# An attention and two mixture-of-experts layers on one core: GpSimd instructions cut in two, and the queues in another order at four places

## The chip, the cores and the metric

One NeuronCore of a Trainium2 chip runs the whole program. The metric is the device time of one execution in microseconds (us); lower is better.

## What is computed

Three layers follow each other, all in float32. The reference, cut to what matters:

```python
# 1. attention, 4 batches x 8 heads, 576 tokens, head size 64
scores = scale * q @ k.T
scores = where(scores >= max(scores) - tau, scores, -1e9)
attn = exp(scores - max(scores)); attn /= sum(attn) + 1e-9
x = (attn @ v)                       # 2304 tokens x 512 columns
# 2. eight experts, each token goes to one
e = argmax(x @ w_gate); gate = softmax(x @ w_gate)[e]
x = gate * (relu(x @ w1[e]) @ w2[e])       # 512 -> 1024 -> 512
# 3. four experts, each token goes to all
p = domain_probs / (sum(domain_probs) + 1e-9)
out = sum over e of p[:, e] * (relu(x @ v1[e]) @ v2[e])
```

## The kernel before

Almost every product of matrices in it is made of three matmuls. A float32 operand is split into a high part, rounded to the fast format (`fp32r`), and a low part, the operand minus the high part. Then high*high + high*low + low*high are summed in PSUM. Each operand is split by two instructions: a copy that rounds, mostly on ScalarE (ACT), and a subtraction on GpSimd (POOL) or VectorE (DVE). Weights arrive as a tile `raw` of 128x1024 and become the tile `hl` (or `v2hl`): high in `hl[:, 0]`, low in `hl[:, 1]`.

All engines run their instructions in the order of the program text (`tc.manual_schedule()`), so the text sets the order, and an instruction that waits holds up those behind it on its engine.

**Attention (0 to about 357 us).** The loop runs over 144 steps `t`, nine for each of 16 head pairs `p`. In step `t`, TensorE makes the scores of the step after (`mm_s`, tile `s`, L733 and L734), transposes of q and k for a later pair (L583), and the transposes of the masked exponentials of four steps ago (`transp`, L781 to L790). VectorE reads the scores (`maxx`, tile `sb`, L742) and two steps later makes the masked row (`mask`, tile `P`, L762). The product with v (PV, L816 and L822) is cut in two halves of tokens per pair, each half of five items: one matmul, and four pairs of matmuls. These ten items wait in a list `pv`. `PG = 3` takes from it every third step, 4, 3 and 3 items. After a half, an item `ev` copies the sum out of PSUM (`outT`, L833, VectorE) in the step that follows, and frees its PSUM bank. When all four pairs of a batch are done, another list `xq` runs the routing (`route`): logits, argmax, places, and a scatter of token rows (`free_scatter`, an indirect DMA issued by POOL).

In steps 140 and 143 the first two weight tiles of layer 2 are split on POOL alone (`dosplit(i, "g", "g")`: L358 makes the high part, L360 the low part).

**Layer 2 (to about 587 us).** 72 units of weights, one tile each; `dosplit(i + 3)` splits a tile three units ahead. The low part is on VectorE for five of eight units and on POOL for the rest.

**Layer 3 (from 588 us).** 48 steps `j`: three phases `ph` of 768 tokens, 16 steps each (four experts by four blocks of the hidden width). In a step, `l1` makes the first matrix product by Strassen's scheme: seven products `prod` of sums of blocks (PSUM tiles X, Y, Z, W, U; L1356 to L1358, six matmuls of 384 columns each), put together on VectorE (`q`, `r`, `c`, L1365) and split for the second product by `relu` (L1370 on ACT, L1371 on VectorE, tile `g`). `l2` makes the second product (L366 to L368, 36 matmuls of 512 columns). The inputs of the seven products are the tiles `yc`: `in_parts` makes high (ACT, L1222) and low (VectorE, L1181) of three blocks and four sums of blocks of `y`. `sums` makes the sums (`t`, and one in place in `y`). Weights for step `j + 2` are prepared by `prep1` (sums `sx` on POOL, L1199 and L1181, splits `hl`), those of the second product by `prep2` (`v2hl`, L1212 and L1181). L1181 is the line of a helper `sub`, used on both engines.

In `l1`, the first product goes to X, ACT copies it to `p` (L1375), and a second product is added into X later, so TensorE waits there for the copy `p`. `mid` is what the caller wants done behind that copy. In step 0 it is `first_blocks`, which makes four of the seven `yc`. The sequence `l1(1)`, `l2(0)`, ... is turned over so that two `l1` stand back to back at three places: steps 1 and 2, 16 and 17, 32 and 33.

The lines that set this order at the places of the change, before:

```python
            if pv and (t % PG == 1 or t > 9 * last):
...
        def first_blocks():
            for _ in range(3):
                next(ahead)
            for _ in parts2(0, (4, 5, 3)):
                pass
            prep2(0)
            next(ahead)
            for _ in parts2(0, (2,)):
                pass
```

## Time and profile before

| | |
|---|---|
| median of 3 runs | 1360.22 us (1359.86 to 1360.77) |
| the profiled execution | 1361.25 us, of which the span of instructions is 1358.8 us |
| TensorE (PE) busy | 1323.6 us, 97% |
| GpSimd (POOL) busy | 890.4 us, 66% |
| VectorE (DVE) busy | 865.9 us, 64% |
| ScalarE (ACT) busy | 653.8 us, 48% |

Times in a row are counted from the start of the span. A row of the timeline is start, duration, engine, line, instruction, and in brackets the idle time of the engine before it and what ended it. A matmul's recorded duration overlaps that of the next, so the pace of TensorE is read from start to start, and its waits from the idle time in brackets. DVE, ACT and POOL rows follow one another in order.

### The profile page before, as it was taken

The page shows a single profiled execution, that of the slowest core. Times are in us where ns is not written, and L with a number is a line of the kernel's source. Part 1 is how long each engine was busy: PE and PEld are TensorE (multiplying, and loading weights), DVE is VectorE, ACT ScalarE, POOL GpSimd, SP SyncE. Part 2 cuts the span into 40 slices and gives each one's busy share as a digit, 9 for nine tenths or more (in the row PEclk, how much of TensorE's full clock was granted, in tenths as well). Part 3 has the DMA queues.
Part 4 walks back from the last instruction along what each step waited for, and adds up shares of the span by engine and source line. Part 5 has one row for each costly group of instructions (what it writes and reads, how often), then busy time and mean ns, then how long its engine had stood idle before and what let it go on. Part 6 is the DMA issues. An engine that isn't in the chain of part 4 may idle for free.

```text
span 1358.8 us, 22300 instructions
## 1 busy us (share of the span) xinstructions
PE 1323.6 (97%) x8120; PEld 1169.4 (86%) x8120; DVE 865.9 (64%) x1705; ACT 653.8 (48%) x1239; POOL 890.4 (66%) x945
## 2 busy tenths in 40 slices
PE   8999999999999999979999999999999999999997
PEld 7777777776899999968999998898999989999986
DVE  8878778777843333545566667666666676655664
ACT  7887786866454455633333334333333343333331
POOL 8876766845385444658666766777677657666642
PEclk8999999999999999989999999999999999999999
DMA  5551111103584556522221112222112222222201
GB/s 153 167 158 57 58 55 62 37 17 110 165 239 148 167 177 203 172 64 78 76 80 62 63 62 67 84 99 78 63 62 76 80 68 80 78 70 78 78 16 47
DMA packets 131696, 127.52 MB, mean 94 GB/s; under 512 B 17920, under 2 KB 110080, under 8 KB 131584
## 3 DMA queue, kind: packets, MB, share of 16 engines
q1 hardware_dynamic: 128128, 116.55, 27.4%
q0 software_dynamic: 3456, 9.51, 1.8%
q8 instruction: 66, 1.08, 0.3%
q14 instruction: 46, 0.38, 0.1%
HBM read 107.61 MB, written 18.42 MB: 93 GB/s over the span
## 4 chain that ended last, share of the span: by engine, by line
PE 68%; issue 3%; POOL 2%; ACT 1%; DVE 1%; POOLq 0%; ACTq 0%; DVEq 0%
PE w L366 14%; PE w L367 14%; PE w L368 14%; PE w L1356 8%; PE w L1358 8%; PE w L1357 8%; PE w L395 1%; PE t L822 0%; DVE g L1371 0%; DVE P L762 0%; POOL out_dram L192 0%; DVE c L1365 0%; POOL hl L360 0%; POOL v2hl L1181 0%; ACT v2hl L1212 0%
## 5 line engine op out<-in xcount | busy, mean ns | idle before, releaser
L1356 PE MATMUL w<-yc,hl 128*128 128x384 f32 x672 | 227.3, 338 | 13.5 <-DVE r L1365 6.5
L1181 POOL TENSOR_TENSOR v2hl<-raw,v2hl 128x1024 fp32r<-128x1024 f32 x48 | 116.0, 2416 | 172.2 <-ACT v2hl L1212 172.2
L1357 PE MATMUL w<-yc,hl 128*128 128x384 f32 x672 | 226.5, 337 | 0.5 <-DVE yc L1181 0.5
L1358 PE MATMUL w<-yc,hl 128*128 128x384 f32 x672 | 226.7, 337 | 0.0
L368 PE MATMUL w<-v2hl,g 128*128 128x512 f32 x576 | 225.3, 391 | 0.0
L366 PE MATMUL w<-v2hl,g 128*128 128x512 f32 x576 | 225.2, 391 | 0.0
L367 PE MATMUL w<-v2hl,g 128*128 128x512 f32 x576 | 224.9, 390 | 0.0
L1420 DVE SCALAR_TENSOR_TENSOR y<-w,big,y 128x512 f32<-128x512 f32 x252 | 179.3, 745 | 51.0 <-PE w L368 50.9
L1370 ACT ACTIVATE g<-c 128x384 fp32r<-128x384 f32 x144 | 75.9, 527 | 191.9 <-DVE c L1365 191.9
L360 POOL TENSOR_TENSOR hl<-raw,hl 128x1024 fp32r<-128x1024 f32 x44 | 107.6, 2446 | 90.6 <-ACT hl L356 55.5
L1371 DVE SCALAR_TENSOR_TENSOR g<-c,g 128x384 fp32r<-128x384 f32 x144 | 111.6, 775 | 62.5 <-ACT g L1370 56.3
L745 POOL TENSOR_SCALAR nm<-nm,sc 128x1 f32<-128x1 f32 x144 | 92.6, 643 | 81.9 <-DVE sb L742 56.0
L1356 PEld LDWEIGHTS w<-yc,hl 128*128 128x128 f32 x672 | 127.0, 189 | 17.3 <-ACT p L1375 7.1
L1212 ACT CAST v2hl<-raw 128x1024 fp32r<-128x1024 f32 x48 | 50.5, 1053 | 188.6 <-PE w L368 188.6
L762 DVE SCALAR_TENSOR_TENSOR P<-sb,nm,E 128x576 f32<-128x576 f32 x144 | 133.5, 928 | 9.1 <-issue 3.0
L1357 PEld LDWEIGHTS w<-yc,hl 128*128 128x128 f32 x672 | 127.1, 189 | 2.6 <-DVE yc L1181 0.8
L368 PEld LDWEIGHTS w<-v2hl,g 128*128 128x128 f32 x576 | 108.3, 188 | 23.6 <-DVE g L1371 0.5
L366 PEld LDWEIGHTS w<-v2hl,g 128*128 128x128 f32 x576 | 108.5, 188 | 21.7 <-ACT g L1370 0.6
L1358 PEld LDWEIGHTS w<-yc,hl 128*128 128x128 f32 x672 | 126.9, 189 | 0.0
L367 PEld LDWEIGHTS w<-v2hl,g 128*128 128x128 f32 x576 | 108.4, 188 | 21.4
L1181 POOL TENSOR_TENSOR hl<-sx,hl 128x1024 fp32r<-128x1024 f32 x48 | 115.6, 2409 | 13.8 <-ACT hl L1196 13.8
L1181 POOL TENSOR_TENSOR hl<-raw,hl 128x512 fp32r<-128x512 f32 x96 | 97.2, 1034 | 41.7 <-ACT hl L1196 41.7
(292 smaller groups left out, 3151.4 us busy)
## 6 DMA issues: line engine op xcount, KB each, us to landing
raw<-in_moe_w_dram SPq DMA_DIRECT2D x168, 512.0 KB
xs<-zrow SPq DMA_DIRECT2D x32, 256.0 KB
xrow<-xs SPq DMA_DIRECT2D x18, 256.0 KB
kt<-in_k_dram SPq DMA_DIRECT2D x16, 256.0 KB
qt<-in_q_dram SPq DMA_DIRECT2D x16, 256.0 KB
vt<-in_v_dram SPq DMA_DIRECT2D x16, 256.0 KB
kt<-in_k_dram SPq DMA_DIRECT2D x16, 32.0 KB
qt<-in_q_dram SPq DMA_DIRECT2D x16, 32.0 KB
```

What stands on the lines that cost most here:

```text
L360: e.tensor_tensor(hl[:, 1, :], raw, hl[:, 0, :].bitcast(F32), op=ALU.subtract)
L366: nc.tensor.matmul(o, lhsT=aH, rhs=bH, start=first, stop=False)
L367: nc.tensor.matmul(o, lhsT=aH, rhs=bL, start=False, stop=False)
L368: nc.tensor.matmul(o, lhsT=aL, rhs=bH, start=False, stop=last)
L745: g.tensor_scalar(nm[:, 1:2], nm[:, 0:1], sc[:, 2:3], None, op0=ALU.add)
L762: nc.vector.scalar_tensor_tensor(P, sb, nm[:, 1:2], e, op0=ALU.is_le, op1=ALU.mult, accum_out=a)
L1181: e.tensor_tensor(o, a, b_, op=ALU.subtract)
L1356: nc.tensor.matmul(o, lhsT=aH, rhs=bH, start=first, stop=False, skip_group_check=True)
L1357: nc.tensor.matmul(o, lhsT=aH, rhs=bL, start=False, stop=False, skip_group_check=True)
L1358: nc.tensor.matmul(o, lhsT=aL, rhs=bH, start=False, stop=last, skip_group_check=True)
L1371: return lambda: nc.vector.scalar_tensor_tensor(o[1], src, 0.0, o[0].bitcast(F32), op0=ALU.max, op1=ALU.subtract)
L1420: nc.vector.scalar_tensor_tensor(d, w3(o), s_, d, op0=ALU.mult, op1=ALU.add)
```

## The change

1. GpSimd's instructions on 1024 columns become two on 512, everywhere (`split`, `parts`, `prep2`).
2. PV: a half of five items is run whole, in steps 0 and 5 of nine, where ten items were spread over three of nine.
3. The Exp of the routing is issued one step of its list earlier.
4. The low parts of the last five weight tiles of layer 2 are on VectorE.
5. In step 0 of layer 3, the last sum of blocks (`t2`) is on VectorE and comes earlier; its high part is made ahead of `prep2(0)`; its low part comes behind `r`, in `last_block`.
6. In steps 1, 16 and 32 the whole of `prep1` and `prep2` goes into `mid`, behind the copy `p`.

```diff
@@ route
-        yield "scatter"
-
         ex = small([128, 5, 8], "ex")[:, :nt]
         nc.scalar.activation(ex, d, AF.Exp)
+        yield "scatter"
+
@@ split
-            nc.gpsimd.tensor_scalar(hl[:, 0, :], raw, 1.0, 1.0, op0=ALU.mult, op1=ALU.mult)
-        e = nc.vector if eL == "v" else nc.gpsimd
-        e.tensor_tensor(hl[:, 1, :], raw, hl[:, 0, :].bitcast(F32), op=ALU.subtract)
+            for c in (slice(0, 512), slice(512, 1024)):
+                nc.gpsimd.tensor_scalar(hl[:, 0, c], raw[:, c], 1.0, 1.0, op0=ALU.mult, op1=ALU.mult)
+        for c in (slice(0, 512), slice(512, 1024)) if eL == "g" else (slice(0, 1024),):
+            e = nc.vector if eL == "v" else nc.gpsimd
+            e.tensor_tensor(hl[:, 1, c], raw[:, c], hl[:, 0, c].bitcast(F32), op=ALU.subtract)
@@ dosplit
-... eL or ("v" if i % 8 < 3 or i in (3, 4) else "g"), i)
+... eL or ("v" if i % 8 < 3 or i in (3, 4) or i >= len(units) - 5 else "g"), i)
@@ attention
-            if pv and (t % PG == 1 or t > 9 * last):
+            if pv and (t % 9 in (0, 5) or t > 9 * last):
                 d = pv[0][2]
-                n = max(1, (d + DX - t) // (1 if t > 9 * last else PG))
-                n = -(-sum(x[2] == d and x[0].__name__ != "ev" for x in pv) // n)
+                n = 5 if t <= 9 * last else -(-sum(x[2] == d and x[0].__name__ != "ev" for x in pv) // max(1, d + DX - t))
@@ prep1, prep2
-            sub(g, c[1][:, m : m + n, :], src, c[0][:, m : m + n, :].bitcast(F32))
+            for x in range(0, n, 4):
+                y_ = min(n, x + 4)
+                sub(g, c[1][:, m + x : m + y_, :], src if n <= 4 else src[:, x:y_, :], c[0][:, m + x : m + y_, :].bitcast(F32))
...
-        sub(nc.gpsimd, hl[:, 1, :], raw, hl[:, 0, :].bitcast(F32))
+        for c in (slice(0, 512), slice(512, 1024)):
+            sub(nc.gpsimd, hl[:, 1, c], raw[:, c], hl[:, 0, c].bitcast(F32))
@@ sums
-                sub(nc.gpsimd if o is t[2] else e, o, a, b_)
+                sub(e, o, a, b_)
@@ l1
             r = add("r", Z, q)
+            if first:
+                first()
@@ first_blocks
-            for _ in parts2(0, (4, 5, 3)):
-                pass
+            for n, _ in enumerate(parts2(0, (4, 5, 3))):
+                if n == 0:
+                    next(ahead)
+            nc.scalar.copy(yc[2][:, 0], tb[0][2])
             prep2(0)
-            next(ahead)
-            for _ in parts2(0, (2,)):
-                pass
-
-        l1(0, first_blocks, True)
+
+        def last_block():
+            sub(nc.vector, yc[2][:, 1], tb[0][2], yc[2][:, 0].bitcast(F32))
+
+        l1(0, first_blocks, last_block)
@@ the loop over j
-            if j:
-                mid = prep1(j + 2)
-            prep2(j + 1)
+
+            if j == 1 or j and i == 0:
+                mid = lambda j=j: (prep1(j + 2)(), prep2(j + 1))
+            else:
+                if j:
+                    mid = prep1(j + 2)
+                prep2(j + 1)
```

The order of VectorE's queue in step 0 of layer 3, before, from the first sum of blocks to `c`. `t_8569`, `y` and `t_8568` are the first three sums, the `yc` rows are low parts of inputs 4, 5, 3 and 2 of the products, `g` is the low part of a `relu`:

```order
L1181 TENSOR_TENSOR t_8569<-y 128x768
L1181 TENSOR_TENSOR y<-y 128x2x384
L1181 TENSOR_TENSOR t_8568<-y 128x768
L1181 TENSOR_TENSOR yc_8551<-t_8568,yc_8551 128x768
L1181 TENSOR_TENSOR yc_8552<-t_8569,yc_8552 128x768
L1181 TENSOR_TENSOR yc_8550<-y,yc_8550 128x768
L1181 TENSOR_TENSOR yc_8549<-t_8570,yc_8549 128x768
L1371 SCALAR_TENSOR_TENSOR g_1_8554<-w,g_0_8553 128x384
L1365 TENSOR_TENSOR q<-w,p_8566 128x384
L1365 TENSOR_TENSOR r<-w,q 128x384
L1365 TENSOR_TENSOR c_8622<-w,r 128x384
```

The same place after the change:

```order
L1181 TENSOR_TENSOR t_8610<-y 128x768
L1181 TENSOR_TENSOR yc_8593<-t_8610,yc_8593 128x768
L1181 TENSOR_TENSOR t_8612<-y,t_8610 128x768
L1181 TENSOR_TENSOR yc_8594<-t_8611,yc_8594 128x768
L1181 TENSOR_TENSOR yc_8592<-y,yc_8592 128x768
L1374 SCALAR_TENSOR_TENSOR g_1_8596<-w,g_0_8595 128x384
L1368 TENSOR_TENSOR q<-w,p_8608 128x384
L1368 TENSOR_TENSOR r<-w,q 128x384
L1181 TENSOR_TENSOR yc_8591<-t_8612,yc_8591 128x768
L1368 TENSOR_TENSOR c_8665<-w,r 128x384
```

The fourth sum (`t_8612`) has come to this queue from POOL's, behind the first `yc`, and the low part of input 2 (`yc_8591`) has moved from ahead of `g`, `q` and `r` to behind them.

The order of ACT's queue at steps 1 and 2 of layer 3, before: the last three `relu` of `l1(1)`, then the copy `p` of `l1(2)` among the casts of the weights:

```order
L1370 ACTIVATE g_0_8725<-c_8770 128x384
L1370 ACTIVATE g_0_8725<-c_8781 128x384
L1370 ACTIVATE g_0_8725<-c_8791 128x384
L1196 CAST hl<-raw 128x512
L1196 CAST hl<-raw 128x256
L1212 CAST v2hl<-raw 128x1024
L1375 COPY p_8825<-w 128x384
L1196 CAST hl<-sx 128x1024
L1370 ACTIVATE g_0_8813<-w 128x384
```

The same place after the change:

```order
L1373 ACTIVATE g_0_8770<-c_8816 128x384
L1373 ACTIVATE g_0_8770<-c_8827 128x384
L1373 ACTIVATE g_0_8770<-c_8837 128x384
L1378 COPY p_8857<-w 128x384
L1196 CAST hl<-raw 128x512
L1196 CAST hl<-raw 128x256
L1196 CAST hl<-sx 128x1024
L1214 CAST v2hl<-raw 128x1024
L1373 ACTIVATE g_0_8845<-w 128x384
```

The copy `p` now stands right behind the `relu` and ahead of all four casts. It is the same at steps 16 and 17, and 32 and 33.

The order of POOL's queue around step 143, before: `nm` is a small instruction of each step, the two `hl` rows split a weight tile for layer 2:

```order
L745 TENSOR_SCALAR nm_5133<-nm_5133,sc 128x1
L745 TENSOR_SCALAR nm_5165<-nm_5165,sc 128x1
L745 TENSOR_SCALAR nm_5188<-nm_5188,sc 128x1
L358 TENSOR_SCALAR hl<-raw 128x1024
L360 TENSOR_TENSOR hl<-raw,hl 128x1024
L191 MEMSET pad 128x1
```

The same place after the change:

```order
L746 TENSOR_SCALAR nm_5135<-nm_5135,sc 128x1
L746 TENSOR_SCALAR nm_5167<-nm_5167,sc 128x1
L746 TENSOR_SCALAR nm_5190<-nm_5190,sc 128x1
L359 TENSOR_SCALAR hl<-raw 128x512 x2
L362 TENSOR_TENSOR hl<-raw,hl 128x512 x2
L191 MEMSET pad 128x1
```

Nothing has moved there; each of the two instructions has become two of half the columns.

## Rows read from the trace of the kernel before

**Rows 1.** The page, part 1: busy time, share and instructions of each engine.

```profile
PE 1323.6 (97%) x8120; PEld 1169.4 (86%) x8120; DVE 865.9 (64%) x1705; ACT 653.8 (48%) x1239; POOL 890.4 (66%) x945
```

**Rows 2.** Waits of TensorE: us in total, times, longest.

```profile
PE w L1356 <- DVE r L1365: 6.5, 1, 6.5
PE w L1356 <- ACT p L1375: 5.9, 4, 2.0
...
PE t L781 <- DVE P L762: 1.6, 1, 1.6
...
PE t L781 <- DVE outT L833: 0.9, 1, 0.9
```

**Rows 3.** Timeline of TensorE, step 0 of layer 3.

```profile
603.44 0.66 PE L1356 MATMUL w<-yc,hl 128*128 128x384 f32 x1 [6.49 <-DVE r L1365]
...
608.46 0.39 PE L366 MATMUL w<-v2hl,g 128*128 128x512 f32 x1
```

**Rows 4.** Stretches: busy us of PE, PEld, DVE, ACT, POOL, granted clock, DMA.

```profile
603.44:608.44 5.00, 5.00 (x12) 3.72 (x13) 3.62 (x7) 2.10 (x5) 0.00 (x0) 0.50 0.00 2
...
628.92:632.33 3.41, 3.41 (x12) 3.41 (x11) 1.18 (x3) 0.87 (x2) 3.41 (x2) 0.50 0.15 18
```

**Rows 5.** Timeline of VectorE, step 0 of layer 3.

```profile
592.71 1.83 DVE L1181 TENSOR_TENSOR yc<-t,yc 128x768 fp32r<-128x768 f32 x2 [0.90 <-ACT yc L1222]
...
600.30 1.40 DVE L1181 TENSOR_TENSOR yc<-t,yc 128x768 fp32r<-128x768 f32 x1 [4.89 <-ACT yc L1222]
601.63 0.55 DVE L1371 SCALAR_TENSOR_TENSOR g<-w,g 128x384 fp32r<-128x384 f32 x1
```

**Rows 6.** Timeline of ScalarE, step 0 of layer 3.

```profile
594.05 1.05 ACT L1212 CAST v2hl<-raw 128x1024 fp32r<-128x1024 f32 x1
599.44 0.83 ACT L1222 CAST yc<-t 128x768 fp32r<-128x768 f32 x1 [4.33 <-POOL t L1181]
```

**Rows 7.** Timeline of GpSimd, step 0 of layer 3.

```profile
597.61 1.79 POOL L1181 TENSOR_TENSOR t<-y,t 128x768 f32<-128x768 f32 x1
...
608.50 2.01 POOL L1181 TENSOR_TENSOR hl<-raw,hl 128x512 fp32r<-128x512 f32 x2 [5.52 <-ACT hl L1196]
```

**Rows 8.** Timeline of ScalarE, steps 1 and 2 of layer 3.

```profile
625.64 0.91 ACT L1196 CAST hl<-raw 128x512 fp32r<-128x512 f32 x2
...
627.40 0.47 ACT L1375 COPY p<-w 128x384 f32<-128x384 f32 x1
```

**Rows 9.** Timeline of TensorE, steps 1 and 2.

```profile
627.92 0.44 PE L1356 MATMUL w<-yc,hl 128*128 128x384 f32 x1 [2.04 <-ACT p L1375]
```

**Rows 10.** Timeline of TensorE, then of ScalarE, steps 16 and 17.

```profile
863.77 0.44 PE L1356 MATMUL w<-yc,hl 128*128 128x384 f32 x1 [1.60 <-ACT p L1375]
...
861.49 0.91 ACT L1196 CAST hl<-raw 128x512 fp32r<-128x512 f32 x2
```

**Rows 11.** End of attention: timelines of VectorE and GpSimd.

```profile
333.42 2.89 DVE L762 SCALAR_TENSOR_TENSOR P<-sb,nm,E 128x576 f32<-128x576 f32 x1
...
332.97 2.73 POOL L360 TENSOR_TENSOR hl<-raw,hl 128x1024 fp32r<-128x1024 f32 x1
```

**Rows 12.** End of layer 2: timelines of GpSimd and VectorE.

```profile
573.82 5.90 POOL L360 TENSOR_TENSOR hl<-raw,hl 128x1024 fp32r<-128x1024 f32 x2 [0.24 <-PE w L368]
...
574.99 2.49 DVE L1181 TENSOR_TENSOR yc<-y,yc 128x768 fp32r<-128x768 f32 x1
```

**Rows 13.** Groups of instructions, shapes apart: busy us, mean ns, idle before.

```profile
L1181 POOL TENSOR_TENSOR v2hl<-raw,v2hl 128x1024 fp32r<-128x1024 f32 x48 | 116.0, 2416 | 172.2 <-ACT v2hl L1212 172.2
...
L1181 POOL TENSOR_TENSOR hl<-raw,hl 128x512 fp32r<-128x512 f32 x48 | 62.2, 1295 | 41.7 <-ACT hl L1196 41.7
```

**Rows 14.** Attention, one PV slot: timelines of TensorE and VectorE; one stretch.

```profile
66.92 1.68 PE L822 MATMUL t<-PT,vt 128*64 128x288 f32 x12
...
68.65 0.46 DVE L833 COPY outT<-t 128x288 f32<-128x288 f32 x1 [0.47 <-PE t L822]
...
80.00:120.00 40.00, 40.00 (x315) 30.80 (x316) 30.45 (x77) 32.19 (x73) 26.09 (x45) 1.00 0.40 120
```

More of the change, by code (lines that the diff above doesn't have):

```diff
@@ L435, in dosplit @@
         if i < len(units):
-            hls[i] = split(raws.pop(i), eH or "a", eL or ("v" if i % 8 < 3 or i in (3, 4) else "g"), i)
+            hls[i] = split(raws.pop(i), eH or "a", eL or ("v" if i % 8 < 3 or i in (3, 4) or i >= len(units) - 5 else "g"), i)
     def value(ap, engines, top):
@@ L466, in attention @@
         DX = 1
-        PG = 3
         NWARM = (36, 3, 3, 3)
@@ L1341, in parts2, with l1 @@
                 yield
-        def l1(j, mid, first=False):
+        def l1(j, mid, first=None):
             if j >= 3 * NS:
```

## The prediction, made before the changed kernel ran

> **What bounds the kernel now.** I read the page's busy times first: TensorE is busy 97% of the span, GpSimd 66%, VectorE 64%, ScalarE 48% [rows 1]. The matmuls themselves are not changed, so the change can gain only where TensorE stands still or runs at half its clock: at most some 35 us of the span, plus what the clock costs. Next, the waits of TensorE [rows 2], which say where: one wait of 6.5 us for `r` on VectorE, four (5.9 us together) for the copy `p` on ScalarE, 1.6 us for the last masked row `P`, 0.9 us for `outT`. Then the timeline around each of the long waits [rows 3, 5 to 11], and the granted clock of the stretches behind them [rows 4]: 0.50, which is the level of 1.2 GHz, against 1.00 (2.4 GHz) nearly everywhere else. The reader is to see that the 6.5 us wait is followed by 5 us at half clock, and the 2.0 us wait of steps 1 and 2 by 3.41 us at half clock, both between 597 and 633 us.
>
> **The change, part by part.**
>
> *Step 0 of layer 3 (parts 1 and 5).* TensorE stops at 603.44 - 6.49 = 596.95 and goes on at 603.44, when VectorE has made `r` [rows 3]. `r` is late because the low part of the last input stands ahead of it on VectorE and starts only at 600.30 [rows 5]; that waits for its high part on ScalarE at 599.44 [rows 6], this for the sum `t` that GpSimd makes from 597.61 in 1.79 us [rows 7], and GpSimd was held by `v2hl`, whose ScalarE cast starts at 594.05 [rows 6]. After the change the sum is on VectorE behind the first low part. Two low parts take 1.83 us there, 0.92 each [rows 5]; at that price the sum runs from 593.6 to 594.6, and the two other low parts end at 596.4. They come 0.9 us later than before, so TensorE's last products ahead of the wait end some 0.5 us later, at 597.5, inside the old wait. ScalarE makes the high part at 594.6 (0.83, to 595.4), then `v2hl` (1.05, to 596.4) [rows 6], then the first `relu` (0.5, estimated from the 0.47 of the copy `p` of the same size in rows 8). `g` on VectorE then starts at 596.9 where it started at 601.63 [rows 5], 4.7 us earlier, and `r` frees TensorE at 603.44 - 4.7 = 598.7. The low part of the last input now comes behind `r`: 0.92 if alone, 1.40 beside GpSimd [rows 5]; the second matmul of that product waits for it, to 599.6 or 600.0. The VectorE queue behind it (the sums `c` and their low parts) is late by the same 1.0 to 1.4 us against `r`, but the whole still runs ahead of the old one: what came at 608.46 [rows 3] comes between 608.46 - 4.7 = 603.8 and 608.46 - 3.5 = 605.0. I take 604.2: a gain of 4.3 us, with 3.5 and 4.7 as bounds. The wait doesn't vanish, it becomes four of about 1 us (for `r`, for the low part, for the `relu` of two `c`).
>
> *Does the clock fall there again?* A wait of 2.04 us in one piece was followed by a fall at steps 1 and 2 [rows 4, 9]; behind the 1.60 us of steps 16 and 17 [rows 10] no wait or pace of the timeline shows one. Four pieces of 1 us among matmuls lie between, so I give it one in two. A fall as long as that of rows 4 costs at most half of 3.41 us, 1.7 us; I subtract 0.8.
>
> *Steps 1, 16, 32 (part 6).* At 625.64 ScalarE is free and makes three casts; the copy `p` starts at 627.40 [rows 8] and TensorE goes on at 627.92 after 2.04 us [rows 9]. With `p` in the place of the first cast it starts at 625.64, 1.76 us earlier, and TensorE goes on at 626.2; 0.3 us of the wait stay. At steps 16 and 17 the first cast starts at 861.49 and the wait is 1.60 [rows 10]: `p` would start then and end 0.47 later, at 861.96, while TensorE had run out only at 863.77 - 1.60 = 862.17 by its recorded ends. All of it goes; that place and its twin at steps 32 and 33 make up the rest of the 5.9 us of rows 2, with the 0.6 us of step 0, which stays. So 1.7 + 1.6 + 1.6 = 4.9, and I add 0.1 for each of the two, since recorded ends overlap the next start: 5.1. Without the long wait the clock should not fall at 628.92 [rows 4]: another 1.6, of at most 1.7. The casts moved behind `p` are for step `j + 2` and for the second product of step `j + 1`; their cover is a whole `l1` and `l2`, over 14 us. Together 6.7; bounds 4.9 (the clock falls all the same) and 6.8.
>
> *End of attention (part 1).* The last row `P` on VectorE takes 2.89 us [rows 11]: it starts at 333.42, GpSimd's subtraction on 1024 columns runs from 332.97 to 335.70, and `P` ends 0.6 after that. The same shows in layer 2: a subtraction of VectorE that starts at 574.99 within a GpSimd instruction takes 2.49 instead of 0.92, while two GpSimd instructions back to back take 5.90, 1.1 more than twice 2.4 [rows 12, 13]. So VectorE waited for the first of them to end and then ran ahead of the second. With two halves, `P` waits for one half at most, 1.29 us by the groups [rows 13], and ends by about 335.0 at the latest rather than at 336.31. TensorE was ready at 336.4 - 1.6 = 334.8 [rows 2]. Gain 1.4, bounds 0 and 1.6.
> The Trainium skill, page SBUF — State Buffer, section Who interferes with whom, has a rule for it: an instruction of VectorE with two inputs in SBUF contends with one of GpSimd that reads SBUF, and whoever issues first keeps the pair of ports for the whole instruction. By that rule the trace agrees; but the rule also lets GpSimd's second half, if it is first in line, shut `P` out again, and then the end of attention would gain nothing (the bound of 0).
>
> *The price of halves (part 1).* 2 x 1295 ns against 2416 ns [rows 13]: 0.17 us more for each of the 48 `v2hl`, as many `sx` parts, and some 40 tiles of layer 2, about 23 us of GpSimd's time in all. GpSimd is idle for over 450 us [rows 1], and waits for ScalarE's casts in layer 3 (172 and 42 us in rows 13), so I cost it at nothing. If that cover were gone, the price would be those 23 us.
>
> *PV in two runs of five (part 2).* Six matmuls of PV, three items, take 1.61 us up to the next score [rows 14], so five items take about 2.7 in one run, twice in nine steps, instead of 2.1, 1.6 and 1.6. The work is the same. Behind the run VectorE waits for its end to copy `outT`, as it does now (0.47 in rows 14), only longer. It can, having 9.5 of 40 us free in that stretch, where TensorE has none [rows 14]. The bank of PSUM is held for one step instead of four, which may remove the 0.9 us for `outT` [rows 2]. I take 0.5, bounds +2 and -2.
>
> *The rest (parts 3 and 4).* An Exp one step earlier on ScalarE, which is 19% idle there [rows 14], and five subtractions from GpSimd to VectorE at the end of layer 2, where VectorE has already waited for GpSimd [rows 12]: nothing.
>
> **The sum.** 4.3 - 0.8 + 6.7 + 1.4 + 0.5 = 12.1 us. The profiled execution took 1361.25 us (span 1358.8 and 2.45 around it), 1.0 over the median of 1360.22; so 1349.1 for it and 1348.1 for the median. I say 1348.
>
> **Rivals.**
> *The clock and the ports don't give in.* TensorE's four short waits let the clock fall in step 0 (1.7 instead of 0.8 lost), the 0.3 us that stay at steps 1 and 2 let it fall there too (5.1 instead of 6.7), and `P` is shut out by the second half (0 instead of 1.4). Then 4.3 - 1.7 + 5.1 + 0 + 0.5 = 8.2: 1352. For it: [rows 4] show two falls within 30 us. Against: the 1.60 us wait without one, and rows 12.
> *GpSimd becomes late.* Layer 3 starts 4.3 us earlier, but GpSimd's `hl` for step 1 waited for ScalarE until 608.50 [rows 7]. If that doesn't move forward with the `relu`s ahead of it, and halves cost 0.5 us up to step 2, `l1(2)` waits and gives back most of the 4.3: 1352 as well. Against: ScalarE's casts stand behind the `relu`s in its queue, which come earlier too.
> *Slower: the long runs of PV starve the scores.* In a run of 2.7 us no score is made; if VectorE, or a bank not yet copied, then holds TensorE for x us, there are 32 such runs. The gain of 11.6 elsewhere is used up at x = 0.36. At x = 0.6 the time would be 1360.2 - 11.6 + 19.2 = 1368. For it: TensorE is full there, so each wait counts. Against: VectorE's slack in rows 14, and its 0.47 wait now shows that VectorE is early, not late, at the end of a slot.
>
> **How the numbers follow.** The forecast 0.72, its own range 1345 to 1351; the clock and ports 0.13; GpSimd late 0.08; slower 0.07. The range: below, the upper bounds (4.7, no fall, 6.8, 1.6, 2) give 15.1, or 1345, and I leave 1 us for what the queues give unasked: 1344. Above, it takes in the second and third case with PV at -2: 1354. Outside lie the slow case and some of the rest. A measurement of this kernel tells about 0.2% (2.7 us) from no change. Faster by more than that: all of the first three and a little less, 0.91; within it 0.04; slower 0.05.
>
> **What would show it.** In the profile after: TensorE's wait for `r` of 6.49 replaced by waits of about 1 us each between 595 and 604 us from start, the clock at 1.00 or one fall there, none at steps 1 and 2; the waits for `p` down to one of some 0.3 and that of 0.6; `P` at the end of attention at under 2 us; attention's own length the same within 2 us. It would be wrong if the waits of TensorE for `sb` or for a PSUM bank grew behind the PV runs, or if layer 3 showed waits for GpSimd.

## The result, and the profile after

The changed kernel took 1339.39 us (median of three runs, 1337.32 to 1340.30) against 1360.22 before: a ratio of 0.9844, 95% interval 0.9821 to 0.9866. The forecast was 1348 with a range from 1344 to 1354, so the time lies below the range. Its sign was right; the gain is 20.8 us instead of 12.1. The profiled execution took 1337.32 us, its span 1335.5.

The page of the changed kernel, part 1, which answers to [rows 1]:

```profile
PE 1312.0 (98%) x8120; PEld 1172.3 (88%) x8120; DVE 866.9 (65%) x1711; ACT 649.9 (49%) x1239; POOL 902.7 (68%) x1076
```

TensorE has the same 8120 instructions, but is busy for 11.6 us less. A change that only removed waits would leave that number as it was, as long as the clock is as often low; between 20 us and the last 7 us of the span it is at 0.50 for 10.2 us in both traces. It is the first sign of what the prediction left out.

Waits of TensorE in the changed kernel (us in total, times, longest), to be read against [rows 2]:

```profile
PE s L734 <- DVE sb L743: 5.5, 9, 2.5
PE w L1359 <- ACT p L1378: 1.5, 2, 0.9
...
PE w L1360 <- DVE yc L1181: 1.2, 2, 0.8
...
PE w L1359 <- DVE r L1368: 1.0, 1, 1.0
```

The wait of 6.5 us for `r` is now 1.0, those for `p` are down from 5.9 to 1.5, and those for `P` and `outT` are gone. New is one of 2.5 us for `sb`, at 37 us:

```profile
37.06 0.40 PE L734 MATMUL s<-kT,qHT 128*128 128x288 f32 x1 [2.52 <-DVE sb L743]
```

*Where the time went by stages.* The first matmul of layer 3 moved from 588.18 to 574.82, 13.4 us earlier; the rest of the span became 9.9 us shorter. The prediction had 10.2 for layer 3 (4.3 - 0.8 + 6.7) and 1.9 for all that lies ahead of it. So it was right for layer 3, and missed 11.5 us ahead of it: 1.0 in layer 2 (its first matmul into `w` moved from 354.54 to 342.13), the rest in attention.

*Step 0 of layer 3*, TensorE of the changed kernel:

```profile
585.77 0.41 PE L1359 MATMUL w<-yc,hl 128*128 128x384 f32 x1 [0.96 <-DVE r L1368]
586.98 0.46 PE L1360 MATMUL w<-yc,hl 128*128 128x384 f32 x1 [0.80 <-DVE yc L1181]
...
591.23 0.39 PE L368 MATMUL w<-v2hl,g 128*128 128x512 f32 x1
```

and VectorE:

```profile
580.75 0.95 DVE L1181 TENSOR_TENSOR t<-y,t 128x768 f32<-128x768 f32 x1
...
585.06 0.56 DVE L1368 TENSOR_TENSOR r<-w,q 128x384 f32<-128x384 f32 x1
585.54 1.39 DVE L1181 TENSOR_TENSOR yc<-t,yc 128x768 fp32r<-128x768 f32 x1
```

The sum `t` is on VectorE, `r` comes before the last low part, and that low part takes 1.39, as forecast. The matmul at 591.23 has the place of the one at 608.46 in [rows 3]: from the first matmul of layer 3 it is 16.41 us instead of 20.28, a gain of 3.9.

*The granted clock.* Stretches of the changed kernel (busy us of each engine, granted clock, DMA), to be read against [rows 4]:

```profile
37.71:41.13 3.42, 3.42 (x17) 2.38 (x17) 3.31 (x13) 2.75 (x6) 2.75 (x15) 0.50 0.39 82
577.02:580.43 3.41, 3.41 (x12) 3.41 (x12) 2.47 (x3) 1.42 (x2) 0.00 (x0) 0.50 0.02 5
587.26:590.67 3.41, 3.41 (x10) 2.42 (x9) 2.77 (x6) 1.31 (x3) 2.69 (x4) 0.50 0.45 150
```

There are two falls in step 0, where before there was one of twice the length (6.8 us from 601.61 on, of which [rows 4] show the 5.0 behind the wait), none at step 1, and a new one behind the wait at 37 us.

*Step 1*, TensorE, then ScalarE, of the changed kernel:

```profile
609.55 0.44 PE L1359 MATMUL w<-yc,hl 128*128 128x384 f32 x1 [0.90 <-ACT p L1378]
...
608.61 0.52 ACT L1373 ACTIVATE g<-c 128x384 fp32r<-128x384 f32 x1 [1.29 <-DVE c L1368]
609.04 0.46 ACT L1378 COPY p<-w 128x384 f32<-128x384 f32 x1
```

`p` now comes right behind the last `relu` and ahead of the casts, but that `relu` itself ends late, so 0.90 us of the 2.04 [rows 9] stay.

*Attention.* Nine steps make a pair. In an undisturbed pair, one without gate or route, VectorE's copy of the scores, `sb`, starts at the first and the last of ten steps at (kernel before, then the changed one):

```profile
L742 DVE TENSOR_SCALAR_CACHE_REDUCE sb<-s x10: 747/754/759, 63.8 to 82.7; 128x576 f32<-128x576 f32 x10
```

```profile
L743 DVE TENSOR_SCALAR_CACHE_REDUCE sb<-s x10: 746/752/758, 65.5 to 83.7; 128x576 f32<-128x576 f32 x10
```

That is 18.9 us for a pair before and 18.2 after. 0.69 in each of 16 pairs would be 11.0, and by the start of pair 15 the changed kernel is 10.8 us ahead, but that the two agree is in part luck. The five undisturbed pairs gain 0.65 to 0.70 each, 3.4 together; pair 1 takes 21.1 us instead of 19.2, with the new wait of 2.5 us in it; and the eight pairs at the ends of batches gain 9.7, more than 0.69 each. There, executions of the same instructions differ by over 1 us: pair 11 takes 21.4 us in this trace of the kernel before, and 20.2 and 20.1 in layer3_only and halves_only below, which change nothing in it. The first run of PV comes at step 14, not 13, so TensorE meets VectorE sooner there.

### The profile page after: what moved, and what is told of

It is laid out like the page before. It is cut to its first block, busy times and chain, and to the rows that moved or that the text cites. A ratio compares the mean times of both kernels' runs of the same rounds, so it can differ in the third digit from the quotient of the medians.

```text
span 1335.5 us, 22456 instructions
## 1 busy us (share of the span) xinstructions
PE 1312.0 (98%) x8120; PEld 1172.3 (88%) x8120; DVE 866.9 (65%) x1711; ACT 649.9 (49%) x1239; POOL 902.7 (68%) x1076
## 4 chain that ended last, share of the span: by engine, by line
PE 52%; issue 2%; POOL 1%; DVE 1%; ACT 0%; POOLq 0%; DVEq 0%
PE w L368 9%; PE w L370 9%; PE w L369 9%; PE w L1359 8%; PE w L1360 8%; PE w L1361 8%; POOL out_dram L192 0%; POOL v2hl L1181 0%; DVE g L1374 0%; DVE t L1181 0%; POOL hl L1181 0%; DVE yc L1181 0%; ACT v2hl L1214 0%; DVE c L1368 0%; ACT g L1373 0%
## 5 line engine op out<-in xcount | busy, mean ns | idle before, releaser
L1181 POOL TENSOR_TENSOR v2hl<-raw,v2hl 128x512 fp32r<-128x512 f32 x96 | 126.8, 1345 | 155.2 <-ACT v2hl L1214 155.2
L362 POOL TENSOR_TENSOR hl<-raw,hl 128x512 fp32r<-128x512 f32 x78 | 99.4, 1296 | 74.1 <-ACT hl L356 50.8
L763 DVE SCALAR_TENSOR_TENSOR P<-sb,nm,E 128x576 f32<-128x576 f32 x144 | 128.2, 891 | 8.8 <-ACT E L752 2.9
L1181 POOL TENSOR_TENSOR hl<-sx,hl 128x512 fp32r<-128x512 f32 x96 | 123.5, 1314 | 11.7 <-ACT hl L1196 11.7
L369 PEld LDWEIGHTS w<-v2hl,g 128*128 128x128 f32 x576 | 108.4, 188 | 21.4
L1181 POOL TENSOR_TENSOR hl<-raw,hl 128x512 fp32r<-128x512 f32 x96 | 97.2, 1034 | 39.4 <-ACT hl L1196 39.4
```

The lines of the kernel that those rows point to most:

```text
L362: e.tensor_tensor(hl[:, 1, c], raw[:, c], hl[:, 0, c].bitcast(F32), op=ALU.subtract)
L369: nc.tensor.matmul(o, lhsT=aH, rhs=bL, start=False, stop=False)
L763: nc.vector.scalar_tensor_tensor(P, sb, nm[:, 1:2], e, op0=ALU.is_le, op1=ALU.mult, accum_out=a)
L1181: e.tensor_tensor(o, a, b_, op=ALU.subtract)
```

## The experiments

Times are medians, each with its ratio to runs of the kernel before on the same chip, and the 95% interval.

### One part, or two, on the kernel before

**pv_only.** The kernel before with part 2.

```
-            if pv and (t % PG == 1 or t > 9 * last):
+            if pv and (t % 9 in (0, 5) or t > 9 * last):
...
```

> The kernel before with part 2 alone (PV in two runs of five). Theory, shape: TensorE pays for each change between stationaries of 128 columns and of 64, and two runs make two stretches of 64 columns in a pair instead of four. In the trace of the changed kernel the distance from score to score over an undisturbed pair went from 18.91 to 18.22 us, so 16 pairs give about 11 us less: 1349 here, 0.991 to 0.993 of before. Rival, elsewhere: the part is worth the 0.5 us of the prediction, and the missing 9 us come from another part or from parts that work together: 1360, a ratio within 0.998 and 1.001.

1354.09 us, 0.9961 (0.9948 to 0.9974): 5.3 us, half of what the shape theory said and ten times what the prediction said. The undisturbed pair is at 18.2 us, as expected. What is missing is lost in pair 1 (21.0 us, as in the changed kernel) and at the ends of the batches. At one of these, in a pair with route, VectorE, with TensorE behind it and ScalarE ahead of it, shows:

```profile
142.50 0.19 DVE L177 TENSOR_REDUCE sg<-ex 128x4 f32<-128x32 f32 x1 [2.50 <-ACT ex L175]
142.60 0.75 DVE L741 TENSOR_SCALAR_CACHE_REDUCE sb<-s 128x576 f32<-128x576 f32 x1
...
143.41 0.40 PE L732 MATMUL s<-kT,qHT 128*128 128x288 f32 x1 [1.45 <-DVE sb L741]
...
142.22 0.24 ACT L175 ACTIVATE ex<-rd 128x32 f32<-128x32 f32 x1
```

route's sum waits 2.50 us for its Exp, which stands on ScalarE behind copies of this step; `sb` waits behind the sum in VectorE's queue, and TensorE for `sb`. Part 3 moves just this Exp.

**route_only**, **pv_and_route.** The kernel before with part 3 alone, and with parts 2 and 3.

```
-        yield "scatter"
         ex = small([128, 5, 8], "ex")[:, :nt]
         nc.scalar.activation(ex, d, AF.Exp)
+        yield "scatter"
```

> The kernel before with part 3 alone (the Exp of route one step earlier). PV in two runs alone gave 5.3 us, and its trace shows VectorE waiting 2.50 us at 142.50 for that Exp, which stands behind copies on ScalarE, with TensorE 1.45 us behind it. Theory, interplay: in the kernel before, VectorE has slack at that place, so the Exp earlier gives nothing there: 1359, a ratio of 0.999 to 1.001. Rival: the Exp alone is worth 4 us with any order of PV: 1355, a ratio of 0.996 to 0.998.

> The kernel before with parts 2 and 3. Theory, interplay: with the Exp earlier, the waits behind it that PV in two runs brought (1.45 us at 143.41, 1.22 and 0.96 at 232 to 234, 1.09 at 311 to 313) go, and the two parts together give 9 to 10 us, where 5.3 and 0 stand for each alone: 1349.5, a ratio of 0.992 to 0.994. Rival: the parts add up, and the rest came from halves or from layer 3 in the changed kernel: 1354, 0.995 to 0.997.

route_only: 1365.18 us, 1.0033 (1.0021 to 1.0045), slower by 4.5. pv_and_route: 1352.15 us, 0.9932 (0.9918 to 0.9945), faster by 9.2. So the parts don't add up: the Exp costs 4.5 us without the runs, and with them it brings 4 (9.2 against 5.3). Both theories on route_only missed its sign. Its rows (VectorE, then TensorE):

```profile
153.18 0.94 DVE L762 SCALAR_TENSOR_TENSOR P<-sb,nm,E 128x576 f32<-128x576 f32 x1 [1.83 <-POOL nm L745]
154.05 0.08 DVE L762 DVE_READ_ACCUMULATOR P<-sb,nm,E 128x1 f32 x1
154.05 0.45 DVE L833 COPY outT<-t 128x288 f32<-128x288 f32 x1
...
154.64 0.42 PE L583 MATMUL t<-identr,qH 128*128 128x128 f32 x3 [2.44 <-DVE outT L833]
```

There `P` waits 1.83 us for `nm` on GpSimd, the copy of `outT` stands behind `P`, and TensorE's transposes wait 2.44 us for the bank of PSUM that this copy frees (0.9 at this place before, [rows 2]). The clock is at 0.50 from 155.38 to 158.80. With PV in two runs, no copy of `outT` stands at that place. How the Exp makes `nm` later is not shown, and the profiled execution, 1362.28 us, is the fastest of six, so these rows need not hold the whole loss.

**layer3_only.** The kernel before with parts 5 and 6.

```
...
+            for n, _ in enumerate(parts2(0, (4, 5, 3))):
+                if n == 0:
+                    next(ahead)
+            nc.scalar.copy(yc[2][:, 0], tb[0][2])
...
+                mid = lambda j=j: (prep1(j + 2)(), prep2(j + 1))
...
```

> The kernel before with parts 5 and 6 alone (step 0 of layer 3, and the casts behind the copy at steps 1, 16 and 32). Theory: the prediction was right here, with 4.3 - 0.8 for step 0 and 6.7 for the other steps; from the first matmul of layer 3 to the end of the span the changed kernel is 9.9 us shorter. So about 10 us less, 1350, 0.992 to 0.994 of before. Rival: layer 3 gained in the changed kernel since the halves of GpSimd's instructions let VectorE in; without them the part gives 7 us or less, a ratio over 0.995.

1349.40 us, 0.9929 (0.9916 to 0.9941): 9.7 us. The theory holds; layer 3 doesn't need the halves.

**halves_only.** The kernel before with part 1.

```
...
-        sub(nc.gpsimd, hl[:, 1, :], raw, hl[:, 0, :].bitcast(F32))
+        for c in (slice(0, 512), slice(512, 1024)):
+            sub(nc.gpsimd, hl[:, 1, c], raw[:, c], hl[:, 0, c].bitcast(F32))
```

> The kernel before with part 1 alone (each instruction of GpSimd on 1024 columns as two). Theory: it shortens the last masked row at the end of attention, 1.4 us less, and costs nothing elsewhere; 1359, a ratio of 0.998 to 1.000. Rival: a large share of the 9 us that the prediction missed comes from VectorE getting in between the halves, in layer 2 and at the end of attention: 1353 or less. If halves cost GpSimd time that somebody waits for, the ratio is over 1.001.

1358.29 us, 0.9997 (0.9989 to 1.0006). TensorE's wait for `P` at the end of attention is gone from its trace, as forecast, but the gain doesn't arrive: in step 0 of layer 3 a wait for `p` is 1.54 us, where the changed kernel has 0.61 (at 576.75) and the kernel before 0.61 too (at 590.11), and the clock is at 0.50 behind it, a fall that the kernel before doesn't have there (TensorE, then the time behind the wait):

```profile
586.19 0.69 PE L1361 MATMUL w<-yc,hl 128*128 128x384 f32 x1 [1.54 <-ACT p L1380]
...
586.19:592.26 6.07, 6.07 (x18) 5.68 (x19) 5.10 (x6) 3.25 (x4) 0.21 (x1) 0.50 0.02 4
```

**low_parts_undone.** The changed kernel without part 4.

```
-eL or ("v" if i % 8 < 3 or i in (3, 4) or i >= len(units) - 5 else "g")
+eL or ("v" if i % 8 < 3 or i in (3, 4) else "g")
```

> The changed kernel with part 4 undone (the last five low parts of layer 2 on GpSimd again). Theory: no change of the time, 1339.4 within 1 us, a ratio of 0.984 to 0.985, since VectorE had waited for GpSimd there. Rival: GpSimd is then late for step 0 of layer 3, whose wait for ScalarE and GpSimd comes back in part: 1341 to 1343, 0.986 to 0.987.

1338.98 us, 0.9835 (0.9822 to 0.9849), against 0.9844 with the part: nothing, as the prediction had it. Its trace is not the same, though: the wait for `p` in step 0 of layer 3 is 1.50 us (at 578.40), about what halves_only has, instead of 0.61, and the clock falls once there instead of twice. So halves and part 4 belong together at that place. (In the kernel before, VectorE makes the low parts of three in eight units of layer 2, 28 of 72, not of five in eight as said above; the five of part 4 were all GpSimd's.)

### What a pair pays

**pv_broken.** Each run of five broken around the transposes of its step.

```
...
+            if len(pv) >= 6 and t % 9 in (0, 5) and t <= 9 * last:
+                for early3 in (1, 2, 3):
+                    pv.popleft()[0]()
             if 0 <= t - LT < NTT:
                 transp(t - LT)
...
```

> The changed kernel, with each run of five items of PV broken in two: the first three stand ahead of the four or six transposes of the same step, the other two behind them. Steps, banks and copies of outT stay as they are; only two more stretches of 64 columns come into each pair. Theory, shape: the 0.69 us of a pair come back, about 11 us in 16 pairs: 1350, a ratio to before of 0.991 to 0.994. Rival, wait: the gain of two runs came from fewer scores delayed or from banks held for a shorter time; breaking a run inside its step changes none of that, and the time stays at 1339, 0.984 to 0.986.

1342.23 us, 0.9877 (0.9863 to 0.9891): 4.5 us come back by the ratio, between the theories. The undisturbed pair goes to 18.5 us, so 0.3 of the 0.69 are the stretches of 64 columns (unbroken rows of matmuls with 64 columns in the stationary), and the rest is something else. The rows of TensorE tell the price of a stretch; they have two records for each matmul of PV. PV of one step in the changed kernel, and in pv_broken:

```profile
66.95 2.16 PE L823 MATMUL t<-PT,vt 128*64 128x288 f32 x16
69.05 0.40 PE L734 MATMUL s<-kT,qHT 128*128 128x288 f32 x1
```

```profile
66.74 1.19 PE L823 MATMUL t<-PT,vt 128*64 128x288 f32 x8
67.86 0.66 PE L782 MATMUL t<-ident,P 128*128 128x128 f32 x4
...
68.67 1.19 PE L823 MATMUL t<-PT,vt 128*64 128x288 f32 x8
69.78 0.41 PE L734 MATMUL s<-kT,qHT 128*128 128x288 f32 x1
```

From the first start to the start of what follows, 16 matmuls take 2.10 us and 8 take 1.12. So 8 more cost 0.98, 0.12 each, and 1.12 - 0.98 leaves 0.14 us, 0.15 by the table below, that each stretch costs whatever its length. It lies at both ends: the records start in twos, and from two to the next two it is 0.24 us within a stretch, 0.29 behind the first two and 0.34 behind the last. That the change of shape makes this, and not the break of a sum as such, is argued: the 0.29 is there behind the 128-column matmul of the same sum (changed kernel) as well as behind transposes (the second stretch of pv_broken).

**banks_held**, **held_two.** The changed kernel with the copy of `outT` four steps, or two, behind its run instead of one.

```
...
+                        due = t + (4 if t <= 9 * last else 1)
-                        dq.append(f)
+                        dq.append((due, f))
...
```

> The changed kernel, where the copy of outT is made four steps behind its run of PV instead of one, so that each sum of PV holds its bank of PSUM for four steps, as before the change; TensorE's order stays as it is but for the late starts of the gate and of route at the four ends of a batch. Theory, banks: of the 0.69 us of an undisturbed pair, 0.36 came from transposes that found a free bank sooner (their steps went from 7.03 to 6.68 us in a pair), and comes back here: pairs of 18.5 to 18.6 us instead of 18.22, some 5 us in all, 1344.5, a ratio of 0.988 to 0.990. Rival, place: the transposes gained since the runs of PV no longer stand beside the transposes of q and k; then pairs stay at 18.2 and the time within 2 us of 1339.

> The changed kernel with the copy of outT two steps behind its run instead of one. With four steps the undisturbed pair went from 18.22 to 19.05 us and the time up by about 15 us. Theory, banks: what costs is a bank that is missing while the transposes of q and k need it, so two steps cost a part of the 0.83 us, 0.1 to 0.4 in a pair, and about 2 to 7 us in all: 1341 to 1346, a ratio of 0.986 to 0.990. Rival, lateness: the time was lost at the four ends of a batch, where gate and route wait for the late copy, and the pair is untouched at two steps: pairs of 18.2.

banks_held: 1355.89 us, 0.9966 (0.9954 to 0.9978), 16 us slower than the changed kernel, three times what the theory said. held_two: 1344.70 us, 0.9887 (0.9871 to 0.9902). Pairs of banks_held, then of held_two:

```profile
L743 DVE TENSOR_SCALAR_CACHE_REDUCE sb<-s x10: 742/752/758, 66.2 to 85.2; 128x576 f32<-128x576 f32 x10
```

```profile
L743 DVE TENSOR_SCALAR_CACHE_REDUCE sb<-s x10: 746/749/758, 63.5 to 81.8; 128x576 f32<-128x576 f32 x10
```

19.0 and 18.3. A bank held for four steps costs 0.83 us a pair; for two steps less than 0.1, so the theory's 0.1 to 0.4 was too much there, and most of held_two's 6 us are lost in one place at the end of a batch, where TensorE waits 2.47 us, with the clock at 0.50 up to 158.03:

```profile
152.80 0.59 PE L584 MATMUL t<-identr,qH 128*128 128x128 f32 x3 [2.47 <-DVE outT L834]
```

Where the 0.83 us sit can be seen in TensorE and ScalarE of banks_held; the profile has no idle time for TensorE there, since recorded ends overlap the next start:

```profile
75.71 0.41 PE L584 MATMUL t<-identr,qH 128*128 128x128 f32 x3
76.22 0.66 PE L782 MATMUL t<-ident,P 128*128 128x128 f32 x4
...
75.45 0.71 ACT L795 COPY PT<-t 128x256 f32<-128x256 f32 x2
```

The three transposes of `q` take 0.51 us up to the next group, where the changed kernel has 0.21 for the same three at 75.33, and the next group starts when ScalarE's copies end (75.45 + 0.71 = 76.16).

The table adds up, over an undisturbed pair, the time from each matmul's start to the next one's, by what it makes; a wait counts for the group ahead of it (pv_ten_4 is below):

| kernel | PV, 64 columns | PV, 128 | transposes of `P` | of `k`, `q` | scores | pair |
|---|---|---|---|---|---|---|
| before | 4.48 | 1.26 | 5.10 | 1.93 | 6.14 | 18.91 |
| changed | 4.18 | 1.26 | 4.91 | 1.77 | 6.10 | 18.22 |
| pv_broken | 4.48 | 1.22 | 4.91 | 1.77 | 6.11 | 18.49 |
| banks_held | 4.18 | 1.26 | 5.05 | 2.16 | 6.41 | 19.06 |
| pv_at_4 | 4.18 | 1.26 | 4.69 | 1.76 | 6.10 | 17.99 |
| pv_4_8 | 4.18 | 1.36 | 4.85 | 2.03 | 6.11 | 18.53 |
| pv_ten_4 | 4.03 | 1.17 | 5.31 | 2.75 | 6.11 | 19.37 |

Of the 0.69 us, 0.30 are in the PV matmuls themselves, come back to the hundredth when the runs are broken, and are two stretches of 0.15: four stretches in a pair make 4.48, two 4.18, and the one of pv_ten_4 4.03. Another 0.35 are in the transposes, which don't come back then, but do when banks are held. In the kernel before, a sum of PV held its bank for four steps. That the 0.35 are those banks fits, but banks_held gives 0.83 and not 0.35, so that share is argued, not shown. A rival for a part of it: in the kernel before, two stretches of a pair follow transposes directly, and the last transpose ahead of them takes 0.20 us to the next start instead of 0.11, which could make 0.19 of the 0.35 a price of the change of shape as well.

### Other places for the runs

**pv_at_4**, **pv_4_8**, **pv_6_1**, **pv_ten_4**, **pv_at_4_ends.** The changed kernel with other steps for PV; pv_ten_4 puts all ten items in one run.

```
-            if pv and (t % 9 in (0, 5) or t > 9 * last):
+            if pv and (t % 9 in (0, 4) or t > 9 * last):
...
+            if pv and (t % 9 in (0, 5 if p in (7, 11) else 4) or t > 9 * last):
```

> The changed kernel with the runs of PV at steps 0 and 4 of a pair instead of 0 and 5. The first pair then starts at step 13, not 14, which should take away TensorE's wait of 2.52 us at 37.06 and the 3.41 us at half clock behind it (some 1.9 us for the pair, by the trace). Theory, shape: at step 4 the transposes ahead of the run have no tile of 64 columns, so one stretch of 64 columns in a pair is not entered through another change; 0.1 to 0.2 us in a pair, 1.6 to 3 us. Together 3 to 5 us below the changed kernel: 1335, a ratio to before of 0.981 to 0.983. Rival: the wait at 37 us only moves, since VectorE is late there for GpSimd's iota and for P, and the place of the run does nothing: 1339.

> The changed kernel with the runs of PV at steps 4 and 8 of a pair. Moving one run from step 5 to 4 brought undisturbed pairs from 18.22 to 18.0 us, since the transposes of step 4 end without a tile of 64 columns; those of step 8 do as well, those of step 0 do not. Theory, shape: another 0.2 us in a pair, pairs of 17.75 to 17.85, 3 us more than with steps 0 and 4, so 1332 to 1335 where the ends of the batches do not take it back: a ratio of 0.979 to 0.982. Rival: the 0.22 us came from the step's other work (the transposes of q and k beside it), and the pair stays at 18.0: 0.983.

> The changed kernel with the runs of PV at steps 6 and 1, both behind transposes without a tile of 64 columns, but two steps later than with 4 and 8. Theory, shape: undisturbed pairs of 17.75 to 17.85 as there. What tells it from steps 4 and 8 is the end of a batch, where gate and route start two steps later, and the first pair, whose PV starts at step 15: TensorE's wait at 37 us should stay or grow from 2.52. Time 1333 to 1338, a ratio of 0.980 to 0.984. Rival: as for steps 4 and 8, 0.984.

> The changed kernel with all ten items of PV of a pair in one run at step 4, the two matmuls of 128 columns first, so that one stretch of 64 columns is left in a pair. Theory, shape: 0.15 us for the stretch and 0.2 for the entry at step 0 less than with steps 0 and 4, pairs of 17.6 to 17.8 us; 6 us below the changed kernel: 1333, a ratio of 0.979 to 0.982. Rival, starving (that of the prediction): TensorE makes no score for 5 us, VectorE stands still and can't catch up, and TensorE then waits for sb or a bank: pairs over 18.3 us, a ratio over 0.985.

> The changed kernel with the runs of PV at steps 0 and 4, but at 0 and 5, as in the changed kernel, in the two pairs 7 and 11 in which route runs and in which steps 0 and 4 lost 3.8 and 1.1 us against 0 and 5 (waits of 1.62 us at 146.00 and 2.93 at 230.37). Theory, place: an undisturbed pair gains 0.22 us by the change of shape, and the loss in those two pairs comes from where the run stands beside route's work on GpSimd and ScalarE; with both kept apart the time is 4 to 6 us under the changed kernel's, 1334.5, a ratio of 0.979 to 0.982. Rival: the waits at route come from TensorE being ahead by then, wherever the run stands; 1337.7 as with 0 and 4 throughout, 0.983 to 0.984.

| kernel | us | ratio | interval |
|---|---|---|---|
| pv_at_4 | 1337.72 | 0.9830 | 0.9817 to 0.9844 |
| pv_4_8 | 1338.53 | 0.9839 | 0.9825 to 0.9852 |
| pv_6_1 | 1339.57 | 0.9842 | 0.9828 to 0.9855 |
| pv_ten_4 | 1345.55 | 0.9887 | 0.9872 to 0.9902 |
| pv_at_4_ends | 1336.67 | 0.9824 | 0.9811 to 0.9837 |

No kernel here is faster than the changed one (0.9821 to 0.9866) by more than the intervals allow, though four have a slightly lower ratio.

pv_at_4 brought the pair to 18.0, as expected, and its first wait of 2.5 us is gone. But the reason, a tile of 64 columns ahead of the run, falls with pv_4_8: its runs are both free of that, and its pair is at 18.5, with PV's 64 columns at 4.18 as in the changed kernel and the transposes 0.4 us longer than in pv_at_4. pv_6_1, free of it too, has pairs of 18.0, not 17.8, and keeps the wait at 37 us (2.53), as expected. What step 4 saved is in the transposes of `P` (4.91 to 4.69), so it is a wait of theirs rather than a change of shape. It can be seen in the changed kernel. There the run of step 5 starts 0.32 us behind the start of the last transpose, and just when a copy of ScalarE has ended (75.74 + 0.69 = 76.43); in step 0 the same place takes 0.11:

```profile
76.17 0.27 PE L790 MATMUL t<-ident,P 128*64 128x128 f32 x1
76.49 0.75 PE L817 MATMUL t<-PT,vl 128*128 128x288 f32 x2
...
75.74 0.69 ACT L786 COPY PT<-t 128x512 f32<-128x512 f32 x1
```

In pv_at_4 the gain went into the end of a batch (VectorE, then TensorE):

```profile
143.11 1.30 DVE L763 SCALAR_TENSOR_TENSOR P<-sb,nm,E 128x576 f32<-128x576 f32 x1 [2.45 <-issue]
...
146.00 0.40 PE L734 MATMUL s<-kT,qHT 128*128 128x288 f32 x1 [1.62 <-DVE sb L743]
```

`P` starts there when GpSimd, which issues four scatters in a row until 142.74, has made `nm` (142.78 to 143.08). In pv_at_4_ends this wait stays (1.64 us) and so does the other (2.92): it is not the run in those two pairs that makes them, so the theory on place falls, and the rival, that TensorE is ahead by then, is left, not tested by itself.

pv_ten_4 is the prediction's rival of starving, and here it comes true in part. VectorE's `sb` over 19 steps, two undisturbed pairs, in pv_ten_4 and in the changed kernel:

```profile
L743 DVE TENSOR_SCALAR_CACHE_REDUCE sb<-s x19: 744/747/758, 46.2 to 84.2; 128x576 f32<-128x576 f32 x19
```

```profile
L743 DVE TENSOR_SCALAR_CACHE_REDUCE sb<-s x19: 746/751/758, 47.6 to 83.7; 128x576 f32<-128x576 f32 x19
```

That is 19.0 us a pair, 1.0 more than with two runs of five, while PV's 64 columns take 0.15 less. The time is lost in the transposes, 8.06 us in a pair instead of 6.68. The sum of TensorE's waits for `sb` goes from 5.5 us in 9 to 8.9 in 22, and it waits 3.5 us in 11 for ScalarE's copies `kT` and `PT`, which do not stand in the changed kernel's list.

## Why the prediction was wrong

*The step that failed* is PV in two runs: "The work is the same", with 0.5 us and bounds of 2. Parts 2 and 3 together are worth 9.2 us, and with 9.2 in place of 0.5 the sum would be 20.8, the measured gain (to the tenth by luck, given the intervals). The prediction looked for the gain in TensorE's idle time, and priced three items at 1.61 us and five at 2.7 by the same rows; but 1.61 us holds the fixed 0.15 of a stretch, and the slots before had four such stretches in a pair. The group "128*64" stood in [rows 14], and that a pair changes between it and "128*128" could have been counted from the order. The Trainium skill, TensorEngine Tiling (Array Packing), section Key Properties, says that a change of tiling mode drains TensorE; the trace agrees in that a stretch costs a fixed 0.15 us, though no run shows that a drain is what costs. This rule spoke for the change, and the prediction had not weighed it. The other half, the 0.35 us in transposes, is not in the waits that the profile lists either. So "at most some 35 us of the span", the idle time and the clock, was no upper bound: 11.6 us of what was gained lay in TensorE's busy time.

*The second step that failed* is "nothing" for part 3. It was costed by ScalarE's free time in an undisturbed stretch [rows 14], while the place that matters is the end of a batch, where VectorE's queue is in order and waits for the Exp: 4 us with PV in two runs, and 4.5 the other way without.

*Right, point by point.*
- Step 0: 3.9 measured, 4.3 - 0.8 forecast. The clock did fall, the case given one in two; it fell in two pieces.
- Steps 1, 16 and 32: the place behind each came earlier by 2.7, 1.6 and 1.7 us, together 6.0 against 6.7. At step 1, 0.90 us of the wait stay instead of 0.3, since the `relu` ahead of `p` ends late; the fall behind it is gone, as forecast.
- End of attention: `P` takes 1.15 instead of 2.89 [rows 11], and TensorE waits for it no more:

```profile
322.22 1.15 DVE L763 SCALAR_TENSOR_TENSOR P<-sb,nm,E 128x576 f32<-128x576 f32 x1
```

From the last scores to layer 2 the changed kernel is 1.6 us shorter, where 1.4 was forecast. Layer 2 is 0.9 us shorter in halves_only as well, and not in the four kernels without halves: a small gain of part 1 that the prediction didn't have.

- Halves cost nothing that the time shows, and part 4 changed nothing; TensorE waited for GpSimd nowhere in layer 3, and the bound of 0 for the ports didn't come. By the Trainium skill, SBUF — State Buffer, section Who interferes with whom, the second half could have kept `P` out; the 1.15 us say that it did not.
- The rivals: the first two gave layer 3 and the end of attention less than they gained. The slower one, starving, came with a run of ten (pv_ten_4), not with five.

*Do the parts make up the whole?* 9.2 (parts 2 and 3), 9.7 (5 and 6) and 0.4 (1) make 19.3, against 20.8 by medians, within the intervals, which reach 1.2 to 1.8 us to either side of each part and 3 us for the changed kernel.

## What to carry to other kernels

Where TensorE is nearly full, the idle time of the profile is not all that can be won: add up start to start by group in a repeating stretch, and look for shapes that change back and forth and for groups that take longer at one place than at another. Keep matmuls of one shape together, in runs short enough that the engine which reads the other results doesn't starve (five items here, not ten), and copy a sum out of its bank soon. Parts of a change that move the same queue are to be priced together: one that costs 4.5 us alone gave 4 beside another.

## What the runs showed of the hardware

- Each stretch of PV's matmuls with 64 columns cost 0.15 us beside the 0.12 us for each record of a matmul: 4.48, 4.18 and 4.03 us in a pair with four, two and one.
- The same wait doesn't always bring the clock down. In the changed kernel TensorE waited 2.52 us at 37.06 and the clock was at 0.50 behind it, as shown above. low_parts_undone, whose attention has the same instructions, has this wait too (2.52 us at 36.89) and stays at 1.00; its pair 1 takes 19.6 us instead of 21.1, so 1.5 us of that pair go with the fall. held_two also has the wait, and stays at 1.00 (TensorE, then the time behind it):

```profile
36.62 0.40 PE L734 MATMUL s<-kT,qHT 128*128 128x288 f32 x1 [2.53 <-DVE sb L743]
...
36.62:41.00 4.38, 4.38 (x32) 2.96 (x33) 4.28 (x14) 3.30 (x8) 3.58 (x16) 1.00 0.31 64
```

In step 0 of layer 3, too, the changed kernel's first fall, at 577.02 behind waits of 0.90 and 0.61, has none beside it in pv_at_4, where both waits are the same.
